# FFN2 of an attention + two-FFN kernel: the turn of 16 of 18 token tiles moved from TensorE to VectorE block transposes and a DRAM trip

## The chip, the cores and the metric

The kernel runs on one core of a Trainium2 chip. The metric is the device time of one launch in microseconds (us), the median of a few runs. The core has five instruction streams that matter here: TensorE (PE, with its weight loads PEld), VectorE (DVE), ScalarE (ACT), GpSimd (POOL) and SyncE (SP), which issues nearly all DMAs. Each engine executes its own list in order, and they wait for each other by semaphores.

## The reference

Windowed attention over q, k, v (4 x 8 heads x 576 tokens x 64), then two feed-forward networks on 2304 tokens of 512 features. All is fp32. The part that the change touches is the last one:

```python
def _moe2_ref(x, w_in, w_out, g_ln):            # x 2304 x 512, w_in 512 x 1024, w_out 1024 x 512
    h = x @ w_in
    e = np.exp(h - np.max(h, axis=-1, keepdims=True))
    sm = e / (np.sum(e, axis=-1, keepdims=True) + 1e-09)
    solu = h * sm
    mu = np.mean(solu, axis=-1, keepdims=True)
    var = np.mean((solu - mu) ** 2, axis=-1, keepdims=True)
    ln = (solu - mu) / np.sqrt(var + 1e-06) * g_ln
    return ln @ w_out
```

The first network (FFN1) is relu(x @ w_in)^2 @ w_out with 2048 hidden features.

## The kernel before

A planner written in Python (class `Plan`) holds every step of the kernel as a task with an engine, an assumed duration, a rank, the tasks it follows and the buffers it takes and gives back. It plays the tasks through once, and the order in which they start there is the order in which the instructions are emitted: each engine's list is fixed when the kernel is built. fp32 products are made of three matmuls (`TERMS`): every operand is split into a high part (ACT, a copy to fp32r) and a low part (DVE, the difference).

FFN2 fills the last third of the program. It goes over 9 pairs of 128-token tiles, function `pair2` for a pair and `behind` for each of its two tiles (k = 0 and 1):

- `load_x` (L1206, SP): the pair's x, two DMAs of 256 KB, into `xr`; DVE makes four sums (`xs`, L1213 to L1218), ACT and DVE split them and `xr` into high and low parts (`xx`, L1228 and L1231).
- `product` (L1249, PE): seven block products of six matmuls make h = x @ w_in for both tiles. Sums between them are kept by ACT (L1255 `p`, L1271) and DVE (L1259, L1263 `u`, and the last three quarters of h at L1274, L1277, L1280). The first six products stand ahead of these last quarters; tile 1 is whole after L1277, tile 0 after L1280.
- `behind`, for each tile (128 tokens on partitions, 1024 features in a row): `max_h` (DVE L1322), `exp_h` (ACT L1327), `solu` (DVE L1331 to L1334), `centered` (ACT L1337, the tile `e` less its mean), `squares` (ACT L1341, only its sum `rstd` is used), `root` (POOL).
- `transposes2` (PE L1350): `e` must have features on partitions to be multiplied by w_out. Eight 128x128 TensorE transposes (matmuls against `ident`) write the tile, turned, into two PSUM banks `ps_lt`.
- `t_high` (ACT L1356) and `t_low` (DVE L1360): the turned tile, a half (four blocks) at a time, split into the operand tile `lnT`.
- `mm_o` (PE L1367): 24 matmuls of 512 columns per tile, 48 per pair, into `ps_o`; `scaled` (ACT L1372) multiplies by `rstd`, `store_o` (SP L1375) writes 256 KB of the output.

On PE, the 42 product matmuls of a pair stand ahead of the 48 `mm_o` matmuls of the pair before it, so that the row of softmax-like steps of one pair runs beside the matmuls of another. Buffers: `e` and `h` are 4 KB per partition from the pool of 16 `wb` buffers; the pool `g` (three buffers of the same size) is used by FFN1 and free in FFN2.

Of the kernel before, what the change touches and what calls it, by code (L numbers as in the profile page):

```python
# [8 lines left out]
F32 = mybir.dt.float32  # L9
# [3 lines left out]
AF = mybir.ActivationFunctionType  # L13
ALU = mybir.AluOpType
# [4 lines left out]
P = 128  # L19
# [77 lines left out]
def kernel(  # L97
# [18 lines left out]
    nc = tc.nc  # L116
    _, NB, HP, _ = q.shape
    NT, DM = out.shape
    DC = DM // P
    KF = w_in.shape[0]  # L120
    KF2 = w2_out.shape[0]
    DFF2 = KF2 * P
# [31 lines left out]
    for half in range(2):  # L154
        rows = slice(BLK * half, BLK * half + BLK)
# [19 lines left out]
    r_dram = [dram.tile([KF, P, n], F32, name=f"r_dram{t}") for t, n in enumerate(HN)]  # L175
    w2_dram = dram.tile([NH2 * DC, P, 512], F32, name="w2_dram")
# [12 lines left out]
    with ExitStack() as c1:  # L189
# [1126 lines left out]
        def behind(k, i, p, rank, rank_o, done):  # L1316
# [22 lines left out]
            def squares():  # L1339
                o["rstd"] = s_p.tile([P, 1], F32, tag="rstd", name="rstd", bufs=4)  # L1340
                S.activation(out=o["h"], in_=o["e"], func=AF.Square, accum_out=o["rstd"])  # L1341

            def root():
                G.tensor_scalar(out=o["rstd"], in0=o["rstd"], scalar1=1.0 / DFF2, scalar2=1e-6, op0=ALU.mult, op1=ALU.add)  # L1344
                G.tensor_tensor(out=o["rstd"], in0=o["rstd"], in1=mhalf, op=ALU.pow)

# [5 lines left out]
            def t_high(hf):  # L1352
                if not ring:
                    ring["l"] = x_p.tile([P, 4, 2, 512], F32R, tag="xa", name="lnT", bufs=1)
                o["l", hf] = ring["l"][:, 2 * k + hf].rearrange("p a (k n) -> p a k n", k=4)
                S.activation(out=o["l", hf][:, 0], in_=o["t"][hf], func=AF.Copy)  # L1356

            def t_low(hf):
                l = o["l", hf]
                V.tensor_tensor(out=l[:, 1], in0=o["t"][hf], in1=l[:, 0].bitcast(F32), op=ALU.subtract)  # L1360
# [20 lines left out]
            r = add("ACT", 1.25, rank + 3, squares, [a], give=["wb"])  # L1381
            p_ = add("PE", TURN, rank_o - (8 if i < NT // P - 2 else 24), transposes2, [a], take=["t", "t"])
            r = add("POOL", 2.0, rank, root, [r, p_], give=["wb"])
            ls = []
            for hf in range(2):
                a = add("ACT", 0.48, rank, lambda hf=hf: t_high(hf), [p_, *l_free.get((k, hf), [])])
                ls.append(add("DVE", 0.60, rank, lambda hf=hf: t_low(hf), [a], give=["t"]))
# [7 lines left out]
        EARLY0, LATE0 = 20, 20  # L1395
# [65 lines left out]
```

## Time and profile before

| | |
|---|---|
| median of 3 runs | 679.11 us (678.86 to 680.86) |
| the profiled execution | 680.59 us, of which the span from first to last instruction is 678.7 us |
| PE busy in the span | 665.5 us, 98% |
| DVE / ACT / POOL busy | 517.8 us (76%) / 411.9 us (61%) / 122.7 us (18%) |
| granted TensorE clock | 0.997 of full speed |

The profile is one execution. A group of instructions is shown with its count, its busy time (overlaps counted once), the mean duration of one and the idle time of its engine just ahead of it. Matmuls are pipelined: one that is listed with 390 ns can follow another after 230 ns, so what a matmul costs is read from start to start, not from its duration. Start times count from the start of the span.

### The profile page before, as it was taken

To read this page: it belongs to the slowest core of one execution; us is meant where nothing else is said; L and a number is where in the kernel's file an instruction comes from. 1 tells how busy PE (TensorE), PEld (TensorE's weight loads), DVE (VectorE), ACT (ScalarE), POOL (GpSimd) and SP (SyncE) were. 2 spreads that over 40 slices of the span, in tenths; PEclk is the share of its full clock that TensorE was granted. 3 is DMA by queue.
4 is the path that set the end of the run, shared out by engine and by line. 5 is a ranking of instruction groups with operands and counts; after the bars stand their busy time and mean duration, and the time that the engine had idled before them with its cause. 6 is when DMAs were issued, how large, how long until landed. Compare 5 with 4: busy or idle time off the path is not lost.

```text
span 678.7 us, 12578 instructions
## 1 busy us (share of the span) xinstructions
PE 665.5 (98%) x4665; PEld 595.4 (88%) x4665; DVE 517.8 (76%) x969; ACT 411.9 (61%) x967; POOL 122.7 (18%) x160
## 2 busy tenths in 40 slices
PE   8999999999899999999999999999999999999997
PEld 4688878888899999999999999998988888888886
DVE  5999989997796886754698989679876667766551
ACT  5877687775464657654655565464774457545652
POOL 1011110114143444331003333300000000000000
PEclk9999999999899999999999999999999999999999
DMA  8775758765544345316723232453201111110001
GB/s 271 250 268 156 221 188 261 223 210 176 173 128 146 128 158 182 125 37 216 237 66 122 79 109 85 144 189 111 79 26 37 63 62 37 43 47 32 31 16 47
DMA packets 58349, 87.86 MB, mean 129 GB/s; under 512 B 5040, under 2 KB 38832, under 8 KB 58288
## 3 DMA queue, kind: packets, MB, share of 16 engines
q1 hardware_dynamic: 57744, 86.79, 39.9%
q8 instruction: 37, 0.61, 0.4%
q10 hardware_dynamic: 544, 0.26, 0.1%
q14 instruction: 24, 0.20, 0.1%
HBM read 63.97 MB, written 23.07 MB: 128 GB/s over the span
## 4 chain that ended last, share of the span: by engine, by line
PE 76%; DVE 9%; DMA 8%; ACT 4%; issue 2%; SPq 1%; ACTq 0%; DVEq 0%
PE ps_h L867 16%; PE ps_o L1367 14%; PE ps_y L984 14%; PE ps_h L1249 12%; PE ps_y L676 4%; PE ps_h L660 4%; PE ps_h L716 3%; PE ps_lt L1350 2%; PE ps_v L495 2%; ACT e L440 2%; DMA wraw<-in_w_out 2%; PE ps_p L468 2%; DMA x_dram<-y 2%; PE ps_s L415 2%; DMA wraw<-in_w_in 1%
## 5 line engine op out<-in xcount | busy, mean ns | idle before, releaser
L984 PE MATMUL ps_y<-g,wb 128*128 128x384 f32 (+1 forms) x960 | 168.7, 326 | 0.0
L984 PEld LDWEIGHTS ps_y<-g,wb 128*128 128x128 f32 x960 | 158.5, 190 | 0.6 <-issue 0.3
L1367 PE MATMUL ps_o<-w2o,lnT 128*128 128x512 f32 x432 | 100.6, 391 | 0.0
L1367 PEld LDWEIGHTS ps_o<-w2o,lnT 128*128 128x128 f32 x432 | 80.4, 188 | 16.2
L594 POOL TENSOR_TENSOR r<-r 128x256 f32<-128x256 f32 (+2 forms) x52 | 47.2, 912 | 245.2 <-ACT r L666 119.1
L609 DVE TENSOR_TENSOR g<-r,g 128x384 fp32r<-128x384 f32 (+2 forms) x84 | 51.1, 612 | 21.9 <-ACT g L606 21.7
L1249 PE MATMUL ps_h<-w2i,xx 128*128 128x512 f32 x243 | 63.7, 393 | 0.8 <-DVE u L1259 0.8
L606 ACT ACTIVATE g<-r 128x384 fp32r<-128x384 f32 (+2 forms) x84 | 42.0, 503 | 29.9 <-PE ps_y L984 18.7
L594 POOL TENSOR_TENSOR u<-u 128x384 f32<-128x384 f32 x48 | 44.9, 940 | 62.1 <-ACT u L591 44.1
L867 PE MATMUL ps_h<-xa,wo 128*128 128x384 f32 x256 | 55.4, 337 | 0.1
L1249 PEld LDWEIGHTS ps_h<-w2i,xx 128*128 128x128 f32 x243 | 44.9, 188 | 9.9 <-DVE u L1259 1.3
L676 PE MATMUL ps_y<-g,wb 128*128 128x512 f32 (+1 forms) x240 | 49.1, 353 | 0.6 <-DVE g L609 0.5
L660 PE MATMUL ps_h<-x,wa 128*128 128x512 f32 (+1 forms) x240 | 48.4, 352 | 0.3 <-ACT r L666 0.2
L867 PEld LDWEIGHTS ps_h<-xa,wo 128*128 128x128 f32 x256 | 44.9, 188 | 0.9 <-issue 0.6
L440 ACT ACTIVATE e<-e,nmax 128x128 f32<-128x128 f32 x112 | 43.5, 392 | 3.7 <-DVE nmax L423 3.5
L660 PEld LDWEIGHTS ps_h<-x,wa 128*128 128x128 f32 x240 | 38.5, 189 | 6.8 <-ACT pt L473 0.5
L676 PEld LDWEIGHTS ps_y<-g,wb 128*128 128x128 f32 x240 | 38.3, 189 | 6.8 <-DVE g L609 0.9
L591 ACT ACTIVATE u<-u 128x384 f32<-128x384 f32 x48 | 25.0, 522 | 28.2 <-DVE u L902 11.8
L1344 POOL TENSOR_SCALAR rstd<-rstd 128x1 f32<-128x1 f32 x18 | 4.2, 233 | 207.2 <-ACT h L1341 206.6
L867 PE MATMUL ps_h<-xb,wo 128*128 128x384 f32 x160 | 36.5, 337 | 0.2
L1249 PE MATMUL ps_h<-w2x,xx 128*128 128x512 f32 x135 | 36.5, 389 | 0.0
L1360 DVE TENSOR_TENSOR lnT<-ps_lt,lnT 128x512 fp32r<-128x512 f32 x36 | 23.4, 686 | 15.1 <-ACT lnT L1356 15.1
(151 smaller groups left out, 1277.4 us busy)
## 6 DMA issues: line engine op xcount, KB each, us to landing
wraw<-in_w_in SPq DMA_DIRECT2D x24, 512.0 KB, 4.4
wraw<-in_w_out SPq DMA_DIRECT2D x24, 512.0 KB, 4.1
vt<-in_v SPq DMA_DIRECT2D x32, 256.0 KB, 3.1
kt<-in_k SPq DMA_DIRECT2D x16, 384.0 KB, 4.5
r_dram<-u SPq DMA_DIRECT2D x32, 192.0 KB, 1.8
r<-r_dram SPq DMA_DIRECT2D x24, 192.0 KB, 4.1
xr<-x_dram SPq DMA_DIRECT2D x18, 256.0 KB, 3.3
out<-o SPq DMA_DIRECT2D x18, 256.0 KB, 2.0
```

The lines of the kernel that those rows point to most:

```text
L440: S.activation(out=o["er"][:, a, w], in_=s, func=AF.Exp, scale=SCALE if begins else 1.0, bias=o["nmax"][:, a, w : w + 1], accum_out=o["sum ...
L591: S.activation(out=o["r"], in_=o["r"], func=AF.Relu)
L594: G.tensor_tensor(out=o["r"], in0=o["r"], in1=o["r"], op=ALU.mult)
L606: S.activation(out=o["g"][:, 0, :N], in_=o["r"], func=AF.Copy)
L609: V.tensor_tensor(out=o["g"][:, 1, :N], in0=o["r"], in1=o["g"][:, 0, :N].bitcast(F32), op=ALU.subtract)
L660: T.matmul(ps[:, :N], wa[kk][:, wi, c * P : c * P + P], xs[t][:, xi, c, n0:n1], start=n == 0, stop=n == 3 * DC - 1)
L676: T.matmul(acc[t, 0][d][:, n0:n1], wb[kk][:, wi, d * P : d * P + P], o["g"][:, xi, :N], start=kk == 0 and n == 0 and n0 == 0, stop=last an ...
L867: T.matmul(to[:, :N], w["t"][:, wi, off + c * P : off + c * P + P], (lo if xi else hi)()[:, c], start=begins and m == 0, stop=m == 5, skip ...
L984: T.matmul(acc[t, half][d][:, :N], wb[kk][:, wi, d * P : d * P + P], q["g"][:, xi, :N], start=pos == 0 and n == 0, stop=pos == KF - 1 and ...
L1249: T.matmul(o[bank], o["xx", k][:, xi, at : at + P], w2i[w, r][wi][0](), start=begins and m == 0, stop=m == 5, skip_group_check=True)
L1360: V.tensor_tensor(out=l[:, 1], in0=o["t"][hf], in1=l[:, 0].bitcast(F32), op=ALU.subtract)
L1367: T.matmul(o["o"], o["l", hf][:, xi, kk % 4, :], w2o[kk][:, wi, :], start=kk == 0 and n == 0, stop=kk == KF2 - 1 and n == 2)
```

## The change

For tiles 0 to 15 (`TURNED` = 2 tiles, the last pair, stay with TensorE) the turn is done in three steps. `blocks2` is one VectorE instruction that transposes the 32x32 blocks of `e` within each group of 32 partitions and writes them into `h`, grouped by the partition group they belong to. `aside` is one DMA on SP that writes `h`, 512 KB, to a scratch tensor `t_dram` in DRAM. `across` is four DMAs on SP that read it back into `l4` (a buffer of the pool `g`), each filling 32 partitions with rows of 1 KB (128 KB a DMA), so that every 32x32 block lands in its place of the turned tile. `t_high` and `t_low` then read `l4` in SBUF where they read PSUM before. `squares` now writes over `e` after the transpose has read it. Nothing else of the computation changes; the assumed times of the new tasks also change the order that the planner emits.

```diff
--- before.py
+++ after.py
@@ -173,6 +173,7 @@
     x2_dram = [dram.tile([P, DC, n * BLK], F32, name=f"x2_dram{t}") for t, n in enumerate(PASSES)]
     xT_dram = [dram.tile([P, DC, n * BLK], F32, name=f"xT_dram{t}") for t, n in enumerate(PASSES)]
     r_dram = [dram.tile([KF, P, n], F32, name=f"r_dram{t}") for t, n in enumerate(HN)]
+    t_dram = [dram.tile([P, DFF2], F32, name=f"t_dram{i}") for i in range(NT // P)]
     w2_dram = dram.tile([NH2 * DC, P, 512], F32, name="w2_dram")
 
 
@@ -1338,11 +1339,34 @@
 
             def squares():
                 o["rstd"] = s_p.tile([P, 1], F32, tag="rstd", name="rstd", bufs=4)
-                S.activation(out=o["h"], in_=o["e"], func=AF.Square, accum_out=o["rstd"])
+                S.activation(out=o["h" if by_pe else "e"], in_=o["e"], func=AF.Square, accum_out=o["rstd"])
 
             def root():
                 G.tensor_scalar(out=o["rstd"], in0=o["rstd"], scalar1=1.0 / DFF2, scalar2=1e-6, op0=ALU.mult, op1=ALU.add)
                 G.tensor_tensor(out=o["rstd"], in0=o["rstd"], in1=mhalf, op=ALU.pow)
+
+            by_pe = i >= NT // P - TURNED
+
+            def blocks2():
+                V.transpose(out=o["h"].rearrange("p (b c j) -> p c b j", b=4, c=KF2), in_=o["e"].rearrange("p (c b j) -> p c b j", b=4, c=KF2))
+
+            def aside():
+                nc.sync.dma_start(out=t_dram[i], in_=o["h"])
+
+            def across():
+                o["l4"] = g_p.tile([P, 4, KF2, P // 4], F32, tag="g", name="l4")
+                rows = P // 4
+                for b in range(4):
+                    nc.sync.dma_start(out=o["l4"][b * rows : b * rows + rows],
+                                      in_=t_dram[i].rearrange("(a p) (b c j) -> b p a c j", a=4, b=4, c=KF2)[b])
+
+            def turned2(hf):
+                if by_pe:
+                    return o["t"][hf]
+                return o["l4"][:, :, 4 * hf : 4 * hf + 4].rearrange("p a c j -> p c a j")
+
+            def parts2(x):
+                return x if by_pe else x.rearrange("p c (a j) -> p c a j", a=4)
 
             def transposes2():
                 o["t"] = [ps_t.tile([P, 4, P], F32, tag="t", name="ps_lt") for _ in range(2)]
@@ -1353,11 +1377,11 @@
                 if not ring:
                     ring["l"] = x_p.tile([P, 4, 2, 512], F32R, tag="xa", name="lnT", bufs=1)
                 o["l", hf] = ring["l"][:, 2 * k + hf].rearrange("p a (k n) -> p a k n", k=4)
-                S.activation(out=o["l", hf][:, 0], in_=o["t"][hf], func=AF.Copy)
+                S.activation(out=parts2(o["l", hf][:, 0]), in_=turned2(hf), func=AF.Copy)
 
             def t_low(hf):
                 l = o["l", hf]
-                V.tensor_tensor(out=l[:, 1], in0=o["t"][hf], in1=l[:, 0].bitcast(F32), op=ALU.subtract)
+                V.tensor_tensor(out=parts2(l[:, 1]), in0=turned2(hf), in1=parts2(l[:, 0].bitcast(F32)), op=ALU.subtract)
 
             def mm_o(hf):
                 if hf == 0:
@@ -1378,13 +1402,20 @@
             a = add("ACT", 1.10, rank, exp_h, [a], take=["wb"])
             a = add("DVE", 1.95, rank, solu, [a])
             a = add("ACT", 1.10, rank, centered, [a])
-            r = add("ACT", 1.25, rank + 3, squares, [a], give=["wb"])
-            p_ = add("PE", TURN, rank_o - (8 if i < NT // P - 2 else 24), transposes2, [a], take=["t", "t"])
-            r = add("POOL", 2.0, rank, root, [r, p_], give=["wb"])
+            if by_pe:
+                r = add("ACT", 1.25, rank + 3, squares, [a], give=["wb"])
+                p_ = add("PE", TURN, rank_o - (8 if i < NT // P - 2 else 24), transposes2, [a], take=["t", "t"])
+                r = add("POOL", 2.0, rank, root, [r, p_], give=["wb"])
+            else:
+                p_ = add("DVE", 1.2, rank, blocks2, [a], port=True)
+                r = add("ACT", 1.25, rank + 3, squares, [p_])
+                p_ = add("SP", 0.8, rank, aside, [p_], late=2.4, give=["wb"])
+                p_ = add("SP", 1.6, rank, across, [p_], take=["g"], late=2.4)
+                r = add("POOL", 2.0, rank, root, [r], give=["wb"])
             ls = []
             for hf in range(2):
                 a = add("ACT", 0.48, rank, lambda hf=hf: t_high(hf), [p_, *l_free.get((k, hf), [])])
-                ls.append(add("DVE", 0.60, rank, lambda hf=hf: t_low(hf), [a], give=["t"]))
+                ls.append(add("DVE", 0.60, rank, lambda hf=hf: t_low(hf), [a], port=not by_pe, give=["t"] if by_pe else ["g"] * hf))
             for hf in range(2):
                 a = add("PE", mm(512), rank_o, lambda hf=hf: mm_o(hf),
                         [a if hf else None, ls[hf], *(ready["2o", 4 * hf + c] for c in range(4))], take=["a"] * (hf == 0))
@@ -1392,7 +1423,7 @@
             a = add("ACT", 0.59, rank_o, scaled, [a, r], take=["r"], give=["a"])
             add("SP", 1.0, rank_o, store_o, [a], late=2.0, give=["r"])
 
-        EARLY0, LATE0 = 20, 20
+        EARLY0, LATE0, TURNED = 20, 20, 2
         l_free = {(k, hf): past[LAST] for k in range(2) for hf in range(2)}
         NPAIR, PAIR2 = NT // P // 2, 7 * M6 + 2 * (TURN + 2 * mm(512))
         for n in range(NPAIR):
```

Three places show what the new order is. The first is **PE** between two pairs in the middle of FFN2 (`ps_h` are the products, `ps_lt` the transposes, `ps_o` the matmuls of `mm_o`). Before:

```order
L1249 MATMUL ps_h_5742<-w2i,xx 128x512 x6
L1350 MATMUL ps_lt<-ident,e_6408 128x128 x8
L1367 MATMUL ps_o<-w2o,lnT 128x512 x48
L1350 MATMUL ps_lt<-ident,e_6623 128x128 x8
L1249 MATMUL ps_h_6139<-w2i,xx 128x512 x3
L1249 MATMUL ps_h_6139<-w2x,xx 128x512 x3
```

After the change:

```order
L1250 MATMUL ps_h_5760<-w2i,xx 128x512 x6
L1391 MATMUL ps_o<-w2o,lnT 128x512 x48
L1250 MATMUL ps_h_6039<-w2i,xx 128x512 x3
L1250 MATMUL ps_h_6039<-w2x,xx 128x512 x3
L1250 MATMUL ps_h_5760<-w2x,xx 128x512 x3
```

Products and `mm_o` now follow each other with nothing between them, and the two groups of eight transposes are gone. (Only at the start it is otherwise: the first six product matmuls of the third pair stand ahead of the first pair's `mm_o`.)

The second is **DVE** at the end of a pair's products, in the same part of the program (`h` are the quarters of h, `nmax` the maxima, `rs` the start of `solu`). Before:

```order
L1274 TENSOR_TENSOR h_6567<-ps_h_5742,u_6559 128x512
L1277 TENSOR_TENSOR h_6567<-ps_h_6139,u_6551 128x512
L1322 TENSOR_REDUCE nmax_6584<-h_6567 128x1
L1280 TENSOR_TENSOR h_6575<-ps_h_5742,u_6551 128x512
L1322 TENSOR_REDUCE nmax_6618<-h_6575 128x1
L1360 TENSOR_TENSOR lnT<-ps_lt,lnT 128x512 x2
L1331 TENSOR_SCALAR rs_6639<-sums_6601 128x1
```

After the change:

```order
L1275 TENSOR_TENSOR h_6755<-ps_h_5760,u_6746 128x512
L1384 TENSOR_TENSOR lnT<-l_6715,lnT 128x512 x2
L1278 TENSOR_TENSOR h_6755<-ps_h_6039,u_6730 128x512
L1384 TENSOR_TENSOR lnT<-l_6735,lnT 128x512 x2
L1281 TENSOR_TENSOR h_6766<-ps_h_5760,u_6730 128x512
L1323 TENSOR_REDUCE nmax_6797<-h_6755 128x1
L1323 TENSOR_REDUCE nmax_6799<-h_6766 128x1
L1332 TENSOR_SCALAR rs_6820<-sums_6802 128x1
```

The low parts (`lnT`) of the pair before now stand in two places: one tile's ahead of L1278, the other's between L1278 and L1281, both ahead of the maxima. Before, those of one tile stood behind the maxima and those of the other earlier, beside the sums. A little further on DVE has the block transposes, each directly behind the `solu` of both tiles:

```order
L1333 RECIPROCAL rs_6657<-rs_6657 128x1
L1334 SCALAR_TENSOR_TENSOR e_6631,total<-e_6631,rs_6657,h_6580 128x1024
L1335 TENSOR_SCALAR nmu<-total 128x1
L1351 STREAM_TRANSPOSE h_6569<-e_6615 128x8x4x32
L1214 TENSOR_TENSOR xs<-xr 128x256
L1215 TENSOR_TENSOR xs<-xr 128x256
L1351 STREAM_TRANSPOSE h_6580<-e_6631 128x8x4x32
L1218 TENSOR_TENSOR xs<-xs,xr 128x256
L1219 TENSOR_TENSOR xs<-xr,xs 128x256
```

Before, the sums `xs` followed `solu` there with nothing between them.

The third is **SP**, in the middle of FFN2. Before, two pairs, with the numbers of the buffers:

```order
L1206 DMA xr_6404<-x2_dram2_108 128x4x128 x2
L1375 DMA out<-o_6479 128x512
L1375 DMA out<-o_6521 128x512
L1206 DMA xr_6596<-x2_dram3_109 128x4x128 x2
L1375 DMA out<-o_6671 128x512
L1375 DMA out<-o_6713 128x512
```

After the change, for one pair (`t_dram` is `aside`, `l` is `across`):

```order
L1354 DMA t_dram_127<-h_6569 128x1024
L1399 DMA out<-o 128x512
L1354 DMA t_dram_126<-h_6580 128x1024
L1399 DMA out<-o 128x512
L1360 DMA l_6715<-t_dram_127 32x4x256 x4
L1360 DMA l_6735<-t_dram_126 32x4x256 x4
L1207 DMA xr<-x_dram_109 128x4x128 x2
```

The load of `xr` now stands behind both tiles' trips, and both output stores stand between the `aside` and the `across` of the first tile.

## Rows read from the trace of the kernel before

**Rows 1.** The page: busy time and share of the span of each engine.

```profile
PE 665.5 (98%) x4665; PEld 595.4 (88%) x4665; DVE 517.8 (76%) x969; ACT 411.9 (61%) x967; POOL 122.7 (18%) x160
```

**Rows 2.** The page: the chain that ended last, by line.

```profile
PE ps_h L867 16%; PE ps_o L1367 14%; PE ps_y L984 14%; PE ps_h L1249 12%; PE ps_y L676 4%; PE ps_h L660 4%; PE ps_h L716 3%; PE ps_lt L1350 2%; PE ps_v L495 2%; ACT e L440 2%; DMA wraw<-in_w_out 2%; PE ps_p L468 2%; DMA x_dram<-y 2%; PE ps_s L415 2%; DMA wraw<-in_w_in 1%
```

**Rows 3.** Window of one pair: stretch, length, busy (instructions) per engine, clock, DMA.

```profile
core 0: us, PE busy (x) PEld busy (x) DVE busy (x) ACT busy (x) POOL busy (x), PEclk, DMA share, GB/s
540.16:562.34 22.18, 22.18 (x109) 18.55 (x108) 15.41 (x30) 12.79 (x22) 1.59 (x4) 1.00 0.15 47
```

**Rows 4.** Line L1350, the transposes: duration ns min/median/max, first and last start.

```profile
L1350 PE MATMUL ps_lt<-ident,e x144: 270/272/273, 488.7 to 666.4; 128*128 128x128 f32 x144
```

**Rows 5.** Timeline of PE, one pair: start, length, instructions.

```profile
540.16 11.14 PE L1367 MATMUL ps_o<-w2o,lnT 128*128 128x512 f32 x48
551.14 1.03 PE L1350 MATMUL ps_lt<-ident,e 128*128 128x128 f32 x8
551.93 0.94 PE L1249 MATMUL ps_h<-w2i,xx 128*128 128x512 f32 x3
...
561.55 1.03 PE L1350 MATMUL ps_lt<-ident,e 128*128 128x128 f32 x8
562.34 0.94 PE L1367 MATMUL ps_o<-w2o,lnT 128*128 128x512 f32 x3
```

**Rows 6.** Timeline of DVE behind the products of that pair.

```profile
561.02 0.69 DVE L1277 TENSOR_TENSOR h<-ps_h,u 128x512 f32<-128x512 f32 x1 [2.66 <-ACT h L1271]
561.74 1.22 DVE L1322 TENSOR_REDUCE nmax<-h 128x1 f32<-128x1024 f32 x1
562.88 0.68 DVE L1280 TENSOR_TENSOR h<-ps_h,u 128x512 f32<-128x512 f32 x1
563.60 1.22 DVE L1322 TENSOR_REDUCE nmax<-h 128x1 f32<-128x1024 f32 x1
564.76 1.29 DVE L1360 TENSOR_TENSOR lnT<-ps_lt,lnT 128x512 fp32r<-128x512 f32 x2
565.96 0.14 DVE L1331 TENSOR_SCALAR rs<-sums 128x1 f32<-128x1 f32 x1
...
569.51 0.42 DVE L1213 TENSOR_TENSOR xs<-xr 128x256 f32<-128x256 f32 x1
```

**Rows 7.** Timeline of ACT: exp and high parts of a pair.

```profile
540.81 1.15 ACT L1327 ACTIVATE e<-h,nmax 128x1024 f32<-128x1024 f32 x1 [2.01 <-DVE nmax L1322]
541.87 0.19 ACT L1327 ACTIVATION_READ_ACCUMULATOR e<-h,nmax 128x1 f32 x1
541.96 1.07 ACT L1356 ACTIVATE lnT<-ps_lt 128x512 fp32r<-128x512 f32 x2
```

**Rows 8.** DMA issues of the whole program: KB each, median us to landing.

```profile
out<-o SPq DMA_DIRECT2D x18, 256.0 KB, 2.0
r<-r_dram SPq DMA_DIRECT2D x16, 128.0 KB, 2.5
wraw<-in_w_in SPq DMA_DIRECT2D x24, 512.0 KB, 4.4
```

**Rows 9.** DMA issues in 452 to 470 us, where FFN1's last loads meet FFN2's first.

```profile
r<-r_dram SPq DMA_DIRECT2D x4, 192.0 KB, 5.4
```

**Rows 10.** Time of an issue on SP, ns min/median/max, by line.

```profile
L1013 SPq DMA_DIRECT2D r<-r_dram x40: 319/382/1018, 157.3 to 457.9; - x40
L1206 SPq DMA_DIRECT2D xr<-x_dram x18: 524/622/664, 455.0 to 597.5; - x18
```

**Rows 11.** Timeline at the start of FFN2, DVE and PE, around the first `mm_o`.

```profile
493.83 0.69 DVE L1277 TENSOR_TENSOR h<-ps_h,u 128x512 f32<-128x512 f32 x1 [1.43 <-PE ps_h L1249]
494.55 1.22 DVE L1322 TENSOR_REDUCE nmax<-h 128x1 f32<-128x1024 f32 x1
495.69 0.68 DVE L1280 TENSOR_TENSOR h<-ps_h,u 128x512 f32<-128x512 f32 x1
495.78 11.14 PE L1367 MATMUL ps_o<-w2o,lnT 128*128 128x512 f32 x48
```

## The prediction

> **What bounds the kernel now.** Read first the busy shares of the page: TensorE is busy for 98% of the span and no other engine for more than 76% [rows 1]. A share is a mean over stages, so the stage that the change touches comes next. The window of one pair of FFN2 lasts 22.18 us, TensorE is busy for all of it, VectorE for 15.41 and ScalarE for 12.79 [rows 3]. Six such periods follow each other alike. In the chain that ended last, FFN2 shows as its matmuls (L1367 14%, L1249 12%) and as the transposes, L1350, 2% [rows 2]. So FFN2 is bound by TensorE alone, and whatever is taken off its list comes off the end, as long as the rest can follow a shorter pair.
>
> What is taken off is small. The duration of a transpose, 272 ns [rows 4], is no price, since they overlap: eight of them start at 551.14 and the next product starts at 551.93; the second eight start at 561.55 and the next matmul at 562.34 [rows 5]. That is **0.79 us for eight**, both times.
>
> **TensorE's part.** 16 tiles x 0.79 = 12.64 us leave its list. The last pair keeps its two groups. A pair then takes 22.18 - 1.58 = **20.60 us**: 10.98 for `mm_o` (540.16 to 551.14) and 9.62 for the products (551.93 to 561.55) [rows 5].
>
> The rules of "VectorE: DVE Perf Modes" in the Trainium skill (section "Rules for kernel authors") speak against the change: transpose 128x128 on TensorE where a PSUM destination will do, as it did here. By that rule alone nothing would be won. The trace says where it stops: the rule weighs one transpose against another, and here the engine that it favours is the only one without idle time.
>
> **VectorE's part.** One block transpose of 128x1024 fp32 per tile; the trace has none. The nearest rows move the same 1024 elements per partition: the maximum takes 1.22 us [rows 6]. I take **1.22**. From above I bound it by twice that, 2.44, in case four-byte blocks go at half rate; below one pass over the elements I see no reason to go. VectorE then has 15.41 + 2.44 = 17.85 us of work in a pair of 20.60, so it does not become the bound by its sum. The low and high parts read SBUF instead of PSUM; VectorE's and ScalarE's 512-wide steps already do both, at nearly one price, and ScalarE has 7.8 us to spare: nothing. `squares` only writes elsewhere: nothing.
>
> **The DRAM trip.** Per tile: a store of 512 KB, then four loads of 128 KB that wait for it. The store: 256 KB of output land in 2.0 us, loads of 512 KB in 4.4 in a busier part [rows 8]; a store in this quiet stage (DMA share 0.15 [rows 3]) is nearer to the first, and I take **3.0**. The loads: 128 KB land in 2.5 us; the worst rows, four loads of 192 KB beside others, in 5.4 [rows 8, 9]. I take **2.5** from the last issue. An issue on SP takes 0.38 us for plain rows and 0.62 for the finest [rows 10]; three more issues ahead of the last are 1.15, at most 1.87. Sum of the four terms, transposing included: 1.22 + 3.0 + 1.15 + 2.5 = **7.87 us**; with every upper end 2.44 + 4.4 + 1.87 + 5.4 = 14.1.
>
> "DMA: Bandwidth & Descriptors" in the Trainium skill (section "Anatomy of one DMA") fits a DMA issued by GpSimd as 2.0 us plus its bytes at 436 GB/s, most of the 2 us being the receipt of the write. An estimate from it is 3.2 us for the store and 2.3 for a quarter, 7.9 in all. For 256 KB it would give 2.6, and this SP queue's row shows 2.0, so by that row the trace is a little quicker.
>
> **Does it fit into a pair?** I place the new order on the clock of one pair of before [rows 5, 6]; VectorE executes in order, so its list is the chain. The quarter L1277 starts at 561.02. Behind it, at the distances at which the rows follow each other: the low parts of the other tile at 561.71, L1280 at 562.91, the maxima at 563.60 and 564.76. The exp of the first tile starts when the first maximum ends, 564.82, and its sum is there 1.25 later [rows 7], at 566.07. From `rs` to the end of both tiles' `solu` are 3.55 us (565.96 to 569.51 [rows 6]): 569.65. The first tile's half of that ends near 567.9, its `centered`, a pass of 1.15 us on ScalarE like the exp [rows 7], near 569.1: in time. Block transpose to 570.87, store landed 573.9, last load issued 575.05 and landed **577.55**. A high part needs 0.53 to 0.6 and a low part some 0.69: the first half could be ready at 578.9. But ahead of it VectorE has the next pair's quarter L1274, at 578.3, so it is ready at 579.65 and both halves at 580.3. TensorE asks for them at 561.55 + 20.60 = **582.15**, and the next pair's L1277 can start no earlier than 581.62. So 2.5 us are spare on TensorE's side and 1.3 on VectorE's, and the trip may grow by **2.2 us** (to some 10 us for the four terms) before it pushes anything. The second tile lands some 2 to 3 us later and is asked for 2.7 us later (twelve matmuls at 0.23).
>
> What waits behind the new waits on SP: the output stores, for which nobody waits before the end, and the load `xr`, which now goes out behind both trips. The second block transpose ends near 572.8 (two sums stand ahead of it), its store lands near 575.8, four issues later, near 577.4, `xr` is issued; the next pair's splits use it behind the two exps, some 5 us after 581.6. Hidden, unless the trips are late by 5 us.
>
> **The start.** The first pair's tiles fall into FFN1's end. TensorE reaches the first `mm_o` at 495.78 - 1.58, plus six products that the new order puts ahead (1.36): 495.56. VectorE starts L1277 at 493.83 - 0.79 = 493.04, then the maximum (1.22) and L1280 stand ahead of the first low part [rows 11]: 493.04 + 0.69 + 1.22 + 0.65 + 0.69 = 496.3. A stall of 0.75 us, and an estimated 0.5 at the second pair, whose tiles start late for the same reason. Together **1.3 us** (0 to 3). At the end the last pair goes as before: its first transposes stand behind 36 `mm_o` matmuls, 36 x 0.23 = 8.2 us after its products, and `centered` is done 569.1 - 561.55 = 7.6 us after them.
>
> **Sum.** 12.64 - 1.3 = 11.3 us. Against the profiled execution, 680.59 us (span 678.7 and 1.9 around it): 669.3. That execution lies 1.48 above the median of 679.11, so the median becomes **667.8 us**, 1.7% less. About 0.3%, 2 us, is what a measurement of this kernel can tell from no change.
>
> **Rivals.**
> - The block transpose takes 2.44 us. VectorE then has 15.41 + 4.88 = 20.29 us of work in 20.60, and its in-order waits no longer fit: with 1 us left of the waits for products and for ScalarE's quarter (the one ahead of L1277 alone is 2.66 now [rows 6]) a pair lasts 21.3. From the third pair to the last there are six periods: 6 x 0.7 = 4.2, and 1 more at the start: 673 us. For it: nothing shows this operation, and two of them stand in VectorE's loop. Against: no row of VectorE's 1024-wide steps goes at half the rate of the others.
> - The trip is somewhat longer than 10 us, by up to 1.6: every excess goes into each of the six periods, since the late low part holds L1277, the maxima and so the next trip. 0.5 to 1.2 us each: 671 to 675.
> - **Slower than before:** the same loop with the trip at the crowded ends. The gain is used up when the excess is 11.3 / 6 = 1.9 us a pair, that is from 12.0 us for the four terms on. With the store at 4.4, the last load at 5.4, issues of 0.62 and the transpose at 1.22 the sum is 12.9, the excess 2.8, and the time 679.1 - 11.3 + 16.8 = 684.6 us. For it: two tiles' trips, two output stores and `xr` share 6 us of the pair, 3.1 MB instead of 1 MB. Against: even then the mean is some 150 GB/s, and single stores here land in 2.0.
> - The excess is near 1.9 and nothing changes: 678 to 681.
>
> **How the numbers follow.** The forecast (666 to 669.5): 0.62. Slow transposes (669.5 to 675): 0.14. A longer trip (669.5 to 677): 0.08. No change: 0.05. Slower: 0.11. Faster by over 0.3%: 0.62 + 0.14 + 0.08 = 0.84; within 0.3%: 0.05; slower: 0.11. The low end, 666.0, is the whole 12.64 off; the high end, 675, takes in the second case and most of the third and leaves out the last two.
>
> **What the profile would show.** Right: the L1350 group has 16 matmuls left; windows of a pair last 20.6 us with TensorE busy for all of them; a block transpose reads 1.2 us; the store lands in about 3 us and the loads in about 2.5; VectorE is busy for some 17.9 us a pair. Wrong: idle time of TensorE ahead of `mm_o` released by VectorE's low part, ScalarE's high part waiting for the DMA of `l4`, or VectorE busy without a gap. The forecast falls if the four terms come to over 10 us.

## The result and the profile after

The changed kernel takes 669.32 us (median; 666.02 to 672.19), the kernel before 678.99 beside it: a ratio of 0.985, with a 95% interval of 0.9804 to 0.9896. A second comparison gave 0.9892 (0.9843 to 0.994). The forecast was 667.8 us in a range of 666.0 to 675.0.

The total times spread by several us, mostly ahead of FFN2, where the order of the instructions is the same in both kernels (the first product starts anywhere from 458 to 467 us in the profiles below). So FFN2 is read by itself in each profile. From its first product to the end of the span it took 678.7 - 464.45 = 214.25 us before and 663.9 - 460.33 = 203.57 after (203.49 in the second profile): **10.7 us less**, where the prediction had 11.3. The experiments use a shorter measure, from the first `mm_o` matmul to the end of the span: 182.92 us before, 173.19 and 173.14 after.

The page of the profile after: busy time by engine (against [rows 1]), the chain that ended last (against [rows 2]), and the two new kinds of DMA with KB each and median us to landing (against [rows 8]).

```profile
PE 650.5 (98%) x4537; PEld 579.4 (87%) x4537; DVE 533.8 (80%) x985; ACT 414.7 (62%) x967; POOL 127.4 (19%) x160
PE 60%; DVE 19%; DMA 8%; ACT 7%; SPq 3%; issue 3%; ACTq 0%; DVEq 0%
PE ps_y L985 21%; PE ps_h L868 18%; DMA l<-t_dram 5%; PE ps_y L677 3%; PE ps_o L1391 3%; PE ps_h L661 3%; SPq L1360 3%; PE ps_h L717 3%; DVE e L1334 3%; PE ps_h L1250 2%; DMA wraw<-in_w_out 2%; PE ps_v L496 2%; ACT e L441 2%; PE ps_s L416 2%; PE ps_p L469 2%
t_dram<-h SPq DMA_DIRECT2D x16, 512.0 KB, 2.7
l<-t_dram SPq DMA_DIRECT2D x64, 128.0 KB, 3.6
```

TensorE is busy for 98% of the span as before, so its share alone tells nothing. The chain does. Before, FFN2 stood in it as matmuls, 14% and 12% [rows 2]. Now `mm_o` has 3% and the products 2%; in their place stand the loads (5%), their issues on SP (3%) and VectorE. TensorE has hardly a gap, and yet much of what the end hangs on in FFN2 is now the trip. The loop has come to a second limit of nearly the same length, as the experiments show.

The new steps by line in the same profile: duration ns min/median/max, then for the DMAs the time to landing in us. L1351 is the block transpose, L1354 the store `aside`, L1360 the loads `across`.

```profile
L1351 DVE STREAM_TRANSPOSE h<-e x16: 1234/1238/1245, 478.2 to 624.1; 128x1024 f32<-128x1024 f32 x16
...
L1354 SPq DMA_DIRECT2D t_dram<-h x16: 319/335/410, 479.5 to 625.4; - x16
...
DMA to landing us min/median/max: 2.6/2.7/3.5
...
L1360 SPq DMA_DIRECT2D l<-t_dram x64: 302/432/926, 482.7 to 630.5; - x64
...
DMA to landing us min/median/max: 3.1/3.6/5.4
```

Three windows, with the columns of [rows 3]: two pairs, from `mm_o` to `mm_o`, and the stretch from the last pair but one's `mm_o` to the end.

```profile
552.13:572.58 20.45, 20.45 (x92) 16.82 (x91) 17.47 (x32) 13.04 (x22) 1.91 (x4) 1.00 0.52 160
572.58:593.73 21.15, 20.73 (x92) 16.82 (x90) 17.46 (x32) 13.14 (x22) 1.91 (x4) 1.00 0.49 147
...
634.85:663.90 29.05, 24.24 (x113) 19.33 (x111) 10.42 (x20) 12.56 (x20) 1.48 (x4) 1.00 0.09 36
```

Pairs now take 20.42 to 21.15 us, 20.64 in the mean of the five from 531.67 to 634.85, against 22.18 [rows 3]; some have a wait in them (0.42 here), which no pair before had. The last stretch is longer than before, 29.05 against 27.61 us.

### The profile page after: what moved, and what is told of

Read it like the earlier page. It is cut to its first block, busy times and chain, and to the rows that moved or that the text cites. A ratio compares the mean times of both kernels' runs of the same rounds, so it can differ in the third digit from the quotient of the medians.

```text
span 663.9 us, 12486 instructions
## 1 busy us (share of the span) xinstructions
PE 650.5 (98%) x4537; PEld 579.4 (87%) x4537; DVE 533.8 (80%) x985; ACT 414.7 (62%) x967; POOL 127.4 (19%) x160
## 4 chain that ended last, share of the span: by engine, by line
PE 60%; DVE 19%; DMA 8%; ACT 7%; SPq 3%; issue 3%; ACTq 0%; DVEq 0%
PE ps_y L985 21%; PE ps_h L868 18%; DMA l<-t_dram 5%; PE ps_y L677 3%; PE ps_o L1391 3%; PE ps_h L661 3%; SPq L1360 3%; PE ps_h L717 3%; DVE e L1334 3%; PE ps_h L1250 2%; DMA wraw<-in_w_out 2%; PE ps_v L496 2%; ACT e L441 2%; PE ps_s L416 2%; PE ps_p L469 2%
## 5 line engine op out<-in xcount | busy, mean ns | idle before, releaser
L595 POOL TENSOR_TENSOR r<-r 128x256 f32<-128x256 f32 (+2 forms) x52 | 49.9, 965 | 239.0 <-ACT r L667 112.2
L610 DVE TENSOR_TENSOR g<-r,g 128x384 fp32r<-128x384 f32 (+2 forms) x84 | 50.8, 609 | 19.1 <-ACT g L607 18.8
L1250 PEld LDWEIGHTS ps_h<-w2i,xx 128*128 128x128 f32 x243 | 45.4, 188 | 10.4 <-DVE u L1260 1.0
L1380 ACT ACTIVATE lnT<-l 128x512 fp32r<-128x512 f32 x32 | 18.4, 624 | 29.2 <-DMA l<-t_dram 29.2
```

What stands on the lines that cost most here:

```text
L595: G.tensor_tensor(out=o["r"], in0=o["r"], in1=o["r"], op=ALU.mult)
L610: V.tensor_tensor(out=o["g"][:, 1, :N], in0=o["r"], in1=o["g"][:, 0, :N].bitcast(F32), op=ALU.subtract)
L1250: T.matmul(o[bank], o["xx", k][:, xi, at : at + P], w2i[w, r][wi][0](), start=begins and m == 0, stop=m == 5, skip_group_check=True)
```

## The experiments

In the text below a pair's two tiles are the **odd** one, whose trip goes out first, and the **even** one. "Pairs" is the mean of the five periods from the third `mm_o` to the eighth; "output stretch" runs from the first `mm_o` to the end.

| kernel | ratio to before (95%) | pairs, us | output stretch, us |
|---|---|---|---|
| before | | 22.19 | 182.92 |
| the change | 0.985 (0.9804 to 0.9896) | 20.64 | 173.19 |
| the change again | 0.9892 (0.9843 to 0.994) | 20.74 | 173.14 |
| no trip | 0.985 (0.9796 to 0.9904) | 20.40 | 170.79 |
| TensorE's transposes too | 1.0031 (1.0005 to 1.0057) | 22.19 | 182.45 |
| store twice | 1.0451 (1.0403 to 1.0499) | 26.06 | 208.03 |
| block transpose twice | 1.0201 (1.0151 to 1.0251) | 23.33 | 191.95 |
| squares elsewhere | 0.9872 (0.9825 to 0.9919) | 20.67 | 173.21 |
| odd low parts later | 0.9914 (0.9883 to 0.9945) | 21.72 | 177.01 |
| the same, store twice | 1.0524 (1.0495 to 1.0552) | 26.35 | 211.29 |
| even low parts later | 0.9822 (0.9785 to 0.9858) | 20.55 | 172.17 |
| the same, store twice | 1.0355 (1.0321 to 1.0389) | 23.94 | 206.29 |
| store cut in four | 0.9941 (0.9922 to 0.996) | 21.40 | 179.49 |
| all 18 tiles | 0.9944 (0.991 to 0.9977) | 20.77 | 181.49 |

### Is the gain TensorE's time?

TensorE makes the transposes again, beside the change:

```diff
+                add("PE", 0.0, rank_o - 8, transposes2, [a])
                 p_ = add("DVE", 1.2, rank, blocks2, [a], port=True)
```

> The changed kernel, in which TensorE also makes the eight transposes of each of the 16 tiles again, at the places where they stood before; nothing reads them, the operands come from the DRAM trip as with the change. Theory (what the change gains is the time of the transposes on TensorE's list, nothing else): pairs are back at 22.2 us, and from the first output product to the end FFN2 takes 183 us as before, against 173.2 with the change. The trip has 1.8 us more room in such a pair, so no wait for it is left in the loop. Rival (part of the gain is the new order): it stays between 174 and 181.

The line of the transposes in this kernel (as [rows 4]), and one pair on TensorE's timeline:

```profile
L1374 PE MATMUL ps_lt<-ident,e x144: 270/272/273, 484.1 to 664.7; 128*128 128x128 f32 x144
```

```profile
560.55 11.14 PE L1391 MATMUL ps_o<-w2o,lnT 128*128 128x512 f32 x48
582.74 11.14 PE L1391 MATMUL ps_o<-w2o,lnT 128*128 128x512 f32 x48
```

Pairs are 22.19 us as before and the output stretch is 182.45, although every tile makes its trip. TensorE waits for no operand in it from the first `mm_o` on. So the whole gain is time taken off TensorE, none of it comes from the order; and in 22.19 us the trip fits.

### What does the trip cost?

```diff
-                nc.sync.dma_start(out=t_dram[i], in_=o["h"])
+                pass
...
-                for b in range(4): nc.sync.dma_start(out=o["l4"][...], in_=t_dram[i]...)
+                o["l4"] = o["h"].rearrange("p (a c j) -> p a c j", a=4, c=KF2)
```

> The DRAM trip left out: the high and low parts read the block-transposed tile where VectorE wrote it, so that the 32x32 blocks are not moved to their places and what is multiplied by w_out is not the turned tile. Same instructions otherwise. FFN2 (from its first product to the end of the span) took 214.25 us before and 203.57 us with the whole change; the transposes alone are worth 12.64 (16 x 0.79), that is 201.6. Theory (the trip is hidden in the loop and costs only at the start and at the end): pairs stay at 20.6 us and FFN2 becomes at most 2 us shorter, 201.6 to 202.5. Rival (the trip is already a limit of the loop): pairs shorter than 20.6 with idle time of TensorE gone, FFN2 below 201.

> The changed kernel again, on the chip of the other three: about 0.985 of the time of before. All theories: FFN2 203.6 us (within 0.3), pairs of 20.6 us; the last pair from its first output product to the end 29.0 us against 27.6 before, if the late landing of the loads there is no accident of one execution.

A window of the kernel without the trip, from `mm_o` to `mm_o`:

```profile
575.45:595.85 20.40, 20.40 (x92) 16.89 (x90) 17.27 (x32) 13.03 (x23) 1.90 (x4) 1.00 0.16 52
```

Five pairs in a row are 20.40 us without a wait. That is the floor of TensorE's list, and it is lower than the 20.60 that the prediction gave it. The trip costs 173.2 - 170.8 = **2.4 us** of the output stretch: 1.2 (in the second profile 1.7) in the five pairs, and 1.2 (0.7) in the last stretch, which is 27.85 us here. FFN2 as a whole is 202.0 us, in the forecast span of 201.6 to 202.5, but the pairs speak for the rival: they got shorter, and about half of the trip's cost lies in them. The total times (0.985 both) could not have shown that.

Where TensorE waits in the five pairs is plain from its weight loads, which go ahead of its matmuls (us in total, times, longest): in the change,

```profile
PEld ps_h L1250 <- ACT p L1256: 1.4, 3, 0.8
```

and in its second profile:

```profile
PEld ps_h L1250 <- ACT p L1256: 2.0, 3, 1.2
```

Before the change and without the trip they have no wait there at all. So TensorE does not wait for the turned tile itself, but for the copy `p`, a ScalarE step of the next pair's products that has become late.

### How much room has it?

The store is made twice; in another kernel the block transpose.

```diff
                 nc.sync.dma_start(out=t_dram[i], in_=o["h"])
+                nc.sync.dma_start(out=t_dram[i], in_=o["h"])
```

> The 512 KB store to DRAM is made twice, one after the other to the same place, so that the loads wait about 2.7 us longer (and an issue, 0.4); nothing else. Theory (the loop is nearly full: with the change VectorE's last product quarter ahead of the second tile's low part still waits 0.36 us for ScalarE, and the prediction put the spare of the trip at 1.3 to 2.2 us, every excess going into each of six periods): pairs of about 21.5 to 23 us, FFN2 longer by 6 x (3.1 - 0.4 to 2.2), 5 to 16 us, with TensorE waiting ahead of its output products. Rival (the trip is off the path of the loop, with several us to spare): pairs stay at 20.6, only start and end grow, FFN2 longer by under 3 us in a first and last tile.

> VectorE makes the block transpose twice (1.24 us more for each of 16 tiles); nothing else. VectorE is busy for 17.6 of 20.6 us in a pair with the change, so 20.1 of 20.6 here. This is also what the prediction's second case (a transpose of 2.44 us) would have been, put at 673 - 667.8 = 5 us. Theory (VectorE's in-order list has no room): pairs of about 21.3 us, FFN2 some 5 us longer. Rival (its waits give way): pairs stay at 20.6, FFN2 longer by 0 to 1.5 us.

Both cost far more than any theory had. For the reason, one circle of the changed kernel, on VectorE, SP and ScalarE in turn (start, length):

```profile
575.64 2.33 DVE L1323 TENSOR_REDUCE nmax<-h 128x1 f32<-128x1024 f32 x2
...
583.51 1.24 DVE L1351 STREAM_TRANSPOSE h<-e 128x1024 f32<-128x1024 f32 x1
...
594.57 1.29 DVE L1384 TENSOR_TENSOR lnT<-l,lnT 128x512 fp32r<-128x512 f32 x2 [0.68 <-ACT lnT L1380]
595.78 0.69 DVE L1281 TENSOR_TENSOR h<-ps_h,u 128x512 f32<-128x512 f32 x1
596.38 2.33 DVE L1323 TENSOR_REDUCE nmax<-h 128x1 f32<-128x1024 f32 x2
```

```profile
582.98 0.34 SPq L1354 DMA_DIRECT2D t_dram<-h  x1
...
584.78 0.32 SPq L1354 DMA_DIRECT2D t_dram<-h  x1
...
585.69 4.24 SPq L1360 DMA_DIRECT2D l<-t_dram  x8
```

```profile
593.90 1.15 ACT L1380 ACTIVATE lnT<-l 128x512 fp32r<-128x512 f32 x2 [0.74 <-DMA l<-t_dram]
```

From the maxima to the end of the even tile's block transpose: 583.51 + 1.24 - 575.64 = 9.11 us. From there to its high part, that is the trip: 593.90 - 584.75 = 9.15. From there over the low parts and L1281 to the next maxima: 2.48. Together **20.74 us**, and TensorE wants 20.40. That the parts add up to the distance of the maxima is no proof, since any parts between them would. What tells is that they leave no room: over the five circles between the maxima at 513.02 and 616.70 the first part is 9.11 to 9.20 and the last 2.48 each time, the trip is 8.72 to 9.54, and at its end ScalarE and then VectorE stand waiting for it (0.74 and 0.68 in the rows). The trip is no branch off the loop but a part of it, since VectorE executes the even tile's low parts ahead of L1281 and of the maxima on which the next trip depends. The spare was nothing.

With the store made twice the same rows read:

```profile
603.08 2.33 DVE L1323 TENSOR_REDUCE nmax<-h 128x1 f32<-128x1024 f32 x2
...
610.95 1.24 DVE L1351 STREAM_TRANSPOSE h<-e 128x1024 f32<-128x1024 f32 x1
...
629.65 2.33 DVE L1323 TENSOR_REDUCE nmax<-h 128x1 f32<-128x1024 f32 x2
```

```profile
614.27 0.40 SPq L1354 DMA_DIRECT2D t_dram<-h  x1
618.34 0.32 SPq L1355 DMA_DIRECT2D t_dram<-h  x1
...
619.23 4.15 SPq L1361 DMA_DIRECT2D l<-t_dram  x8
```

```profile
627.18 1.15 ACT L1381 ACTIVATE lnT<-l 128x512 fp32r<-128x512 f32 x2 [1.07 <-DMA l<-t_dram]
```

9.11 + 14.99 + 2.47 = 26.57 us. The first and last parts are the same; the trip is 5.8 longer, twice what the edit was meant to add, because SP issues in order: the loads of both tiles stand behind both second stores. All of it goes into this period (in the mean the pairs grew by 5.4). TensorE's slow clock behind long waits, told below, lengthens the matmuls beside that.

With the block transpose made twice the even tile's path is 2.5 us longer (both tiles' transposes stand ahead of its store), and pairs grew by 23.33 - 20.69 = 2.6. Here TensorE waited elsewhere as well. The squares wait for the second transpose, the copy `p` stands behind them on ScalarE, and a product needs `p` (the rows are ScalarE's and TensorE's):

```profile
556.02 1.06 ACT L1342 ACTIVATE e<-e 128x1024 f32<-128x1024 f32 x1 [1.35 <-DVE h L1352]
...
557.08 0.58 ACT L1256 ACTIVATE p<-ps_h 128x512 f32<-128x512 f32 x1
```

```profile
557.71 0.96 PE L1250 MATMUL ps_h<-w2x,xx 128*128 128x512 f32 x3 [1.58 <-ACT p L1256]
```

### Is it the squares, or the circle?

The changed kernel has a wait for `p` too, so the squares were a rival for what is left.

```diff
-                S.activation(out=o["h" if by_pe else "e"], in_=o["e"], func=AF.Square, ...)
+                S.activation(out=o["h"] if by_pe else g_p.tile([P, DFF2], F32, tag="g", name="junk"), in_=o["e"], func=AF.Square, ...)
```

> The sum of squares writes its unused squares into a free buffer and not over the tile that VectorE's block transpose still reads, so that it no longer waits for that transpose, nor what stands behind it on ScalarE (the copy p, for which TensorE waited up to 0.74 us with the change). Buffers of one pool are taken in another order, else nothing. From the first output product to the end it is 173.2 us with the change and 170.8 without the trip. Theory squares (the wait of p behind the squares is what is left of stalls in the loop): 172 or less, no wait of TensorE for p. Theory loop (the second tile's low part is late, it holds the maxima and so everything behind, p too): 173 to 173.5, the waits move elsewhere.

The output stretch stays at 173.21 us, with the clock at 1.00 in all of it (the execution is longer ahead of FFN2, whose first product starts at 467.19), and 0.7 us of waits for `p` remain. Freeing the squares gives nothing. What is left is that all of ScalarE's list behind the maxima is late, and `p` with it; this fits the circle, but this run by itself does not show it.

### Can the circle be opened?

A first try ordered low parts behind the next maxima:

```diff
             a = add("DVE", 1.20, rank, max_h, done)
+            for t in lows.get(i - 1 - k, []):        # low parts of the pair before
+                t["after"].append(a)
```

> On VectorE the second tile's low parts are ordered behind the two maxima of the next pair, not ahead of the last product quarter; the planner gets that one rule more and nothing else. Theory loop (the trip of the second tile, its low part, the maxima and the next trip form a circle as long as a pair): pairs of 20.4 us without waits, and from the first output product to the end 171 to 171.8 us against 173.2 with the change and 170.8 without the trip, so that the whole gains 1.4 to 2.2 us on the change. Theory squares: 173, as with the change. In both a loss is possible if the low parts now come late for TensorE: they would start near 600.4 where TensorE asks at 602.5 in the run of the change.

> As the run before this one, but each tile's store is made twice, one after the other: the trip becomes some 6 us longer, as it did with the change's own order (there the loads went out 8.8 us after the first store instead of 2.7, and pairs took 25 to 27 us instead of 20.5). Theory loop: with the low part of the second tile behind the maxima the circle is open, so the excess no longer goes into each period in full: TensorE waits for the second tile alone, pairs clearly under 25, from 21 to 24. Rival (the trip as such is too slow for a pair, whatever the order): 25 to 27 again.

The index was wrong for the purpose: `i - 1 - k` is the odd tile, whose trip is the earlier one and which TensorE asks for first. TensorE's waits for operands in the output stretch then are (us in total, times, longest):

```profile
PE ps_o L1391 <- DVE lnT L1384: 2.3, 7, 0.6
PE ps_o L1391 <- ACT lnT L1380: 1.8, 4, 0.9
```

Pairs became 1.0 us longer, and the store made twice cost as much as in the change's own order. Neither run bears on the question that it was made for.

The second try takes the even tile, puts its `mm_o` behind all of the odd tile's, and the odd tile's block transpose ahead of the even tile's `solu`:

```diff
+            for t in lows.get(i - 2 - k, []):
+                t["after"].append(a)
...
+                if k: lows["solu", 0]["after"].append(p_)
...
-                behind(k, i, o, rank + LATE0 * (n == 0), rank_o + k * 2 * mm(512), ...)
+                behind(k, i, o, rank + LATE0 * (n == 0), rank_o + (1 - k) * 2 * mm(512), ...)
```

> The tile whose rows go out second (the even one of a pair) gets its low parts behind both maxima of the next pair, which the earlier try did to the other tile; its output matmuls stand behind all 24 of the odd tile (before: behind 12 of them); and on VectorE the odd tile's block transpose stands ahead of the even tile's solu. The planner moves other VectorE and ScalarE steps with that. Theory loop (the even tile's trip, its low parts, the maxima and the next trip form a circle as long as a pair): now the circle has 2 to 3 us to spare, pairs are 20.4 us each without waits, and from the first output product to the end it is 171 to 172 us, against 173.2 with the change and 170.8 without the trip. Rival (the order does not matter, the DMA rows themselves are too slow beside each other): 173 or more, waits of TensorE for the low parts remain.

Three things are changed at once here, and the planner moves other steps with them, so the run can show that the order counts, but not which of the three does it. TensorE's only wait in FFN2 by its matmuls, the chain by line, and the two kinds of DMA:

```profile
PE ps_h L1250 <- DVE u L1260: 0.2, 1, 0.2
```

```profile
PE ps_y L985 19%; PE ps_h L868 18%; PE ps_o L1391 14%; PE ps_h L1250 12%; PE ps_y L677 6%; PE ps_h L661 6%; PE ps_h L717 3%; PE ps_v L496 3%; PE ps_s L416 2%; PE ps_p L469 2%; ACT e L441 1%; PE ps_warm L1445 1%; DVE g L610 1%; DVE w2i L326 1%; DMA r_dram<-u 1%
...
t_dram<-h SPq DMA_DIRECT2D x16, 512.0 KB, 3.0
l<-t_dram SPq DMA_DIRECT2D x64, 128.0 KB, 2.9
```

The waits for `p` are gone. Every other pair still takes 20.7 us, and the weight loads tell why; in the pair from 548.98, on VectorE and TensorE:

```profile
554.07 1.29 DVE L1384 TENSOR_TENSOR lnT<-l,lnT 128x512 fp32r<-128x512 f32 x2
554.81 0.77 PEld L1391 LDWEIGHTS ps_o<-w2o,lnT 128*128 128x128 f32 x4 [0.43 <-DVE lnT L1384]
```

In these pairs the even tile's low parts stand behind the odd tile's `solu`, and a weight load of `mm_o` waits 0.43 us for them; in the others they stand ahead of it and nothing waits. The chain runs through FFN2's matmuls again (14% and 12%), and FFN2 takes 659.5 - 458.35 = 201.15 us against 203.5. The loads land in 2.9 us, now that SP issues the two tiles' loads four and four, some 6 us apart, and not eight in a row. The output stretch, 172.17, misses the forecast by 0.2. The total, 666.29 us, is clearly below the kernel before, but its interval overlaps those of the change: that it is the better one rests on the stretch alone.

> The order of the run before this one, with each store to DRAM made twice in series, some 3 us more for the odd tile and up to 6 for the even one. With the change's own order that made pairs of 25 to 27 us and 208 us from the first output product to the end. Theory loop: 2 to 3 us of it are hidden now, pairs of 21.5 to 24 us, 180 to 198 us in all. Rival (order does not matter): 25 to 27 us again, 205 or more.

Here the expectation failed in part. Pairs, 23.94 us, lie in its range of 21.5 to 24, but the output stretch of 206.3 us is the rival's: the last period takes 20.96 us, where it took 14.19 with the same edit in the change's order, so the end gave back most of what the pairs had won. Pairs are 2.1 us shorter than with the same edit in the change's order, still 3.4 above those without it. VectorE's waits for high parts in the new order, with the store once and twice:

```profile
DVE lnT L1384 <- ACT lnT L1380: 7.6, 4, 3.8
```

```profile
DVE lnT L1385 <- ACT lnT L1381: 43.5, 16, 5.1
```

From the end of the even tile's block transpose to its high part it is 607.97 to 621.02, 13.05 us, against 583.87 to 592.77, 8.90, with one store. Of these 4.1 us a pair shows 3.4, so that some 0.7 were hidden and not the 2 to 3 that I had put; the slow clock behind TensorE's waits is in that. The even low parts now stand behind the maxima but ahead of a `solu` of the same pair, so that by VectorE's order the circle closes one step further on; no run tests this second circle. The order takes most of the waits away; it does not make the trip a side matter.

### A trip cut otherwise, and all tiles

```diff
-                nc.sync.dma_start(out=t_dram[i], in_=o["h"])
+                for q4 in range(4): nc.sync.dma_start(out=t_dram[i]... [q4], in_=o["h"][32 rows] ...)
...
-                for b in range(4): nc.sync.dma_start(out=o["l4"][32 rows], in_=t_dram[i]... [b])
+                nc.sync.dma_start(out=o["l4"]..., in_=t_dram[i])
```

> The change's own order, but the trip is cut otherwise: the store is four DMAs of 128 KB that lay the rows in DRAM in their final order, and one load of 512 KB in rows of 4 KB follows. SP then issues two loads per pair and not eight, which took 4.2 us, and the even tile's load no longer stands behind four others. Theory loop: the even tile's trip is 1 to 2 us shorter, pairs are 20.4 us without waits of TensorE, 171.5 to 172.5 us from the first output product to the end. Rival (the length of the trip is not what is left): 173 and more. If eight stores issue slower than eight loads did, nothing is won and the run decides nothing.

```profile
t_dram<-h SPq DMA_DIRECT2D x64, 128.0 KB, 2.4
l<-t_dram SPq DMA_DIRECT2D x16, 512.0 KB, 5.0
```

The trip did not get shorter: the even tile's store takes four issues, 2.10 us where it took 0.32, and the load of 512 KB behind it lands in 5.0. So the run is no test of a shorter trip. In one circle (maxima at 584.38, end of the block transpose 593.49, high part 603.84, maxima again at 606.54) the trip lasts 10.35 us and the circle 22.16; pairs are 21.40 in the mean.

```diff
-        EARLY0, LATE0, TURNED = 20, 20, 2
+        EARLY0, LATE0, TURNED = 20, 20, 0
```

> All 18 tiles turned by VectorE and DRAM, the last pair too. TensorE loses 1.8 us more, but in the last pair no matmuls of a next pair hide the trip: its output matmuls wait for maxima to low part. In the changed kernel the last pair's transposes stand behind 36 output matmuls, 8.2 us after its products; the row of steps up to the block transpose takes as long, and the trip's 7 to 9 us come on top. Theory: 5 to 9 us more in the last stretch, 178 to 182 us from the first output product to the end, so that half of the gain is gone. Rival: the trip finds cover, 172 to 174.

```profile
658.24 14.21 PE L1391 MATMUL ps_o<-w2o,lnT 128*128 128x512 f32 x48 [7.46 <-ACT lnT L1380]
```

As expected, 181.5 us: the last pair's trip lies open, TensorE waits 7.46 us, and the matmuls behind the wait take 14.21 us in place of 11.04.

## Why the prediction was right, and where not

- **TensorE's term** was too small: 0.79 us for eight transposes. The floor of 20.40 us is 90 matmuls at 0.2267. 48 of them would take 10.88, but the first transpose starts 10.98 behind the first `mm_o` [rows 5], so the switch costs 0.1 that my reading of the start times left out. The price is (22.18 - 20.40) / 2 = **0.89 us**, 14.2 us for 16 tiles and not 12.64.
- **The 20.60 us of a pair** were measured (20.64), but by two errors that cancel, which is luck: the floor is 20.40, and some 0.24 are waits that I had not foreseen.
- **The block transpose:** 1.24 us where I took 1.22. The bound of 2.44 was not needed.
- **The trip's terms:** the store lands in 2.7 us (I took 3.0). The loads land in 3.6, not 2.5, and eight issues take 4.24 us in the rows above, 0.53 each, not 0.38. The two tiles' loads meet, and I had priced them one tile at a time.
- **The spare of 2.2 us** is the step that failed. For the even tile I asked only when TensorE wants it ("lands some 2 to 3 us later and is asked for 2.7 us later"). Its low parts stand ahead of L1281 and of the maxima, as the order in the section on the change shows, and so the even tile closes the circle. By the prediction's own times that circle would still have had room: from the maxima at 563.60 to the block transpose's end at 572.8 are 9.2 us, from there to the last load, issued at 577.4 and landed 2.5 later, 7.1, and with the 2.48 to the next maxima it comes to 18.8, 1.8 below 20.60. The trip took 9.15 in place of 7.1, by the issues and landings of the loads, and with that the room was gone. So two things failed together: a path that I had not followed to its end, and the price of the loads on it. That the loss is small is luck: the circle, 20.74 us, lies just above TensorE's 20.40.
- **Two signs of being wrong** that the prediction names did appear, though the time lies in its range. For the even tile the four terms come to 1.24 + 9.15 = 10.4 us, over the 10 at which the forecast was to fall, and ScalarE's high parts waited for the loads (us in total, times):

```profile
ACT lnT L1380: 29.2, 14
```

- **The start** was about right in size, but not in place: I had put 0.75 us ahead of the first `mm_o`, and the loss stands behind it. From the first `mm_o` to the second are 84 matmuls, 19.04 us, and it took 19.92; the next period took 21.04 for 20.40. That is 1.5 us, where I had 1.3. Without the trip it is as much (19.89 and 21.05): the late tiles cost it, not the trip. The run-up to the first `mm_o` was 0.5 us quicker than its work would make it.
- **The end as before** was wrong: 29.05 and 28.52 against 27.61 us. TensorE waits there for ScalarE, 0.47 us ahead of a group of `mm_o` in both profiles and 0.44 more ahead of a transpose in the first; 0.2 us more stands in the kernel without the trip too (27.85).
- **The rivals:** that each excess goes into each period is shown, and with a harsher price than mine. The slow transpose, put at 673 us, would have been near 690 (the kernel with two transposes measured 690.61). The slower case was nearer than it looked: a trip longer by 5.8 us gave 707 us.

Sum: 14.2 us off TensorE; the start (1.5, less 0.5 of the run-up), the circle (1.2) and the end (1.4) give 3.6 of it back; 10.7 remain, where I had 12.64 - 1.3 = 11.3.

## What to carry to other kernels

When work moves off the busiest engine into a longer path beside it, look for the circle: follow the engine's in-order list from the result of the path to the first step of its next round, and add it up once around. If it comes near the period, every later us in it costs a us in each period, whatever the idle shares say. And price queued transfers for all that are in flight together, the last in line above all.

## What the runs showed of the hardware

TensorE's granted clock fell behind its longer waits. In the kernel with the store made twice TensorE waited 3.46 us ahead of the `mm_o` at 598.97 (columns as in [rows 3]):

```profile
593.00:595.50 2.50, 2.50 (x12) 1.74 (x10) 0.00 (x0) 0.00 (x0) 0.00 (x0) 1.00 0.62 215
595.50:599.00 3.50, 0.04 (x2) 0.03 (x1) 0.05 (x1) 0.71 (x2) 0.00 (x0) 0.91 0.92 241
599.00:602.00 3.00, 3.00 (x7) 2.10 (x8) 2.58 (x5) 2.08 (x4) 0.00 (x0) 0.50 0.70 184
602.00:605.00 3.00, 3.00 (x9) 2.35 (x8) 3.00 (x4) 0.68 (x1) 0.00 (x0) 0.50 0.01 3
605.00:608.00 3.00, 3.00 (x14) 2.49 (x13) 2.64 (x9) 3.00 (x7) 0.00 (x0) 0.97 0.00 0
```

It went from 2.4 to 1.2 GHz for some 6 us, and the 48 matmuls took 14.24 us in place of 11.04. So that wait cost nearly twice its length. Behind a wait of 0.73 us in the same kernel, ahead of the `mm_o` at 546.02, the clock stayed at 1.00. The change's own waits are of that kind: the longest by its matmuls are 0.47 us, and 0.74 for `p` in the second profile, all at 1.00. Even so they cost more than their idle time. The pair with a wait of 0.42 us lasted 21.15, 0.75 over the floor of 20.40, and the one with 0.74 lasted 21.45, 1.05 over. Matmuls overlap, so the idle time between them is less than what the list loses; the waits of the weight loads (1.4 and 2.0 us in the five pairs, which lost 1.2 and 1.7) come nearer.

A load of 512 KB in rows of 4 KB landed in 5.0 us; with its issue of 0.88 that is 5.9, against 5.7 for four loads of 128 KB in rows of 1 KB (four issues of 0.53 and 3.6 to land). Larger rows gave no shorter trip here.
